# A transformer block on one core: token chunks of 2, 2, 4, 4 and 4 tiles instead of 2, 4, 4, 4 and 2, smaller idle products, and another written-out order

## The chip, the core and the metric

The kernel runs on one core of a Trainium2 chip. The metric is the device time of one execution in microseconds, as the median of several runs. The engines have short names: PE is TensorE (PEld its weight loads), DVE is VectorE, ACT is ScalarE, POOL is GpSimd, and SP only issues transfers.

## The reference, cut to what matters

2048 tokens with 448 features pass through an attention block with 16 heads of 28 features and then through a gated feed-forward block with 1792 inner features.

```python
def _A_ref(x, wqkv, w_phi, wo):
    q, k, v = split(x @ wqkv)                       # 16 heads of 28
    phi_q = concat([softmax(q @ w_phi), softmax(-(q @ w_phi))])
    phi_k = concat([softmax(k @ w_phi), softmax(-(k @ w_phi))])
    kv, z = einsum("bhsf,bhsd->bhfd", phi_k, v), einsum("bhsf->bhf", phi_k)
    o = (phi_q @ kv) / (phi_q @ z + 1e-6)
    return o.reshape(B, S, D) @ wo
def _B_ref(x, w_gate, w_up, w_down):
    return (sigmoid(x @ w_gate) * (x @ w_up)) @ w_down
h  = x + _A_ref(layernorm(x), wqkv, w_phi, wo)
h2 = h + _B_ref(layernorm(h), w_gate, w_up, w_down)
```

The sum over all tokens in kv stands between the two halves of the attention: no token can leave it before all tokens have gone into it.

## The kernel before, in words

The 2048 tokens are 16 tiles of 128. The kernel is a graph of tasks, each one or a few instructions on one engine; line 106 is the method that adds them. The order of all tasks is not found at run time: PLAN (line 30) is a list of task numbers written out by hand or by a search. `planned` (line 113) walks it, and `emit` (line 147) puts each task on its engine's queue in that order with semaphore waits for what it needs. A number with a tail such as `57.7-7` also says which of the eight PSUM banks the task writes; whoever takes a bank waits for those who last read it. A number with `~` takes the task's other engine. So an engine works strictly in the order of PLAN, and a task that waits holds up all that stand behind it on its engine, SP's transfers too.

The work runs in these stages.

- **Start** (lines 419 to 503). Five products with ones (L426) keep PE busy while the first weights land. Then the query and key weights are transposed on PE with a column that gives their mean (L445, "WT"), centred on ACT (L460), and folded with the small matrix w_phi (L475, "fold"); the folds leave PSUM by casts on ACT (L483) or DVE (L486). L491 ("csum") makes the column sums of the value weights. The first two token tiles are transposed on PE as well (L552, "xP"), the others by transfers (L363).
- **Keys and values** (lines 569 to 634). For each pair of tiles PE computes keys and values in half-array products (`pair`, line 520: two products of 64 rows run side by side, then called 64-row mode; all others use all 128 rows). ACT takes two exponentials of the key (L599) and a copy of the value (L604); DVE sums (L612) and inverts (L615); POOL, or DVE, multiplies ("phi", L619); PE adds into one bank over all tiles ("kv", L632). On DVE the multiplications with `lock=True` do not run beside POOL: line 126 makes each wait for POOL's task before it in PLAN, and POOL's next for it.
- **Queries** (lines 644 to 690). The same for queries, with POOL adding halves ("hs", L668), DVE reducing (L671), and POOL or DVE multiplying ("em", L681); a transfer turns each result ("eT", L689).
- **Leaving the attention** (lines 695 to 766). DVE copies the sums out ("kvz", L696). Then for each tile: the product with them ("num", L705), reciprocal and division on DVE (L713, "o" L715), a transpose (on PE for tiles 0 and 1, L723; by a transfer otherwise, "oT", L736), and the product with wo ("wo_", L750 for the first two tiles).
- **Second layernorm** (lines 768 to 815). DVE adds to the residual ("h", L770) and takes the statistics (L773, L775), POOL computes the factor (L776, L778, L789), ACT or DVE applies it ("hn", L791 or L793; L785 for the first two tiles), and a transpose brings it into the layout for PE ("hP" L800 and "hT" for tiles 0 and 1, by a transfer for pairs of tiles otherwise, "hT" L812).
- **Feed-forward** (lines 825 to 885). The tiles are taken in chunks given by SIZES (line 225). For each chunk, and for each of 14 blocks of 128 inner features, PE computes gate and up ("gu", also with `half`, L514) with 512 columns for a chunk of four tiles and 256 for one of two; ACT takes tanh (L848, "tg"), DVE multiplies (L855, "hh"). When all 14 blocks are there, each tile's product with w_down ("dn", L874) runs, DVE adds it to the residual ("fin", L881), and a transfer writes it out (L883). A chunk can start only when the "hT" of all its tiles have landed. The last two tiles are split in two column parts with `last` (line 861), so that less stands behind the last product.

Lines 817 to 820 make spare products with ones ("dm"). PLAN uses as many of them as it likes; they write a free bank and compute nothing.

Of the kernel before, what the change touches and what calls it, by code (L numbers as in the profile page):

```python
# [10 lines left out]
P = 128  # L11
# [19 lines left out]
23 24 25 26 27 28 29 30 31 32 33 34 35 36 37 38 39 40 41 42 0 20 18 21 16 17 6 14 8 49 4 57.7-7 58 59 60 61 654.0-0  # L31
64.0-0 3 65 9 5 15 43 1 11 10 44 2 51 46 45 48 47 55 73.1-1 74 19 22 66 75 67.2-2 70.3-3 68 69 120 71 72 118 119 121
12 62 63 122 7 13 123 124 167.4-4 94.5-5 165.6-6 97.7-7 88.0-0 98 95 89 91.1-1 92 99~ 90~ 96~ 166 168 93 112.2-2 113
169.3-3 171 173 175 170.6-6 172 174 176 193.0-7 79.4-4 180 179 127 125 115 128 114 126 182 80 183 187 186 177.1-5
194 189 132 190 136 133 138 134 137 139 135 178 76.2-2 195.3-6 129 130 131 184 116 191 140 117 141 198 181 81 197
188 205 204 185.4-4 85.1-1 196 211.0-5 206 199 82.7-7 192 212 213.3-6 77 200 142 86 201 207 83 208 215 216 87 218
145 219 147 143 146 149 148 144 150 202 209 220 151 152 214 84 78 217 229.0-1 222 203 230 234 223 224 225 226 227
153 231.2-7 233 210 240 236 106.3-3 232 100.5-5 107 108 235 241 101 247.0-6 221 242 102 248 251 103.3-3 109.2-2 104
252 154 237 243 244 156 254 255 157 158 160 159 161 155 238 110 228 249.1-7 250 111 105 239 265.0-5 260 258 245 259
253 319.2-3 266 270 269 320 256 162 163 246 261 262 263 164 257 272 276 277 327 328 273 279 274 267.6-7 283.0-1 268  # L40
271 284 329 280 287 288 330 290 291 278 321 322 281 331 285.3-5 286 301.0-6 302 264 275 335.2-7 282 336 292 294 295
306 305 289 293 323 297 298 324 308 312 313 315 309 316 332 299 325 310~ 317~ 326~ 54 56 50 52 53 334 333 296 338
337 303.0-1 353.3-6 304 314 344 307 345 354 370.2-5 300 363 355 311 356 362 318 455 387.0-1 461.7-7 388 346 339 347
462 348 340 463 364 365 341 366 397 371 372 519.4-4 404.3-6 389 390 464.7-7 456.0-0 465 520 515.7-7 349 357 358 457
458 359 350 342 367 343 360 459.0-0 405 521 379 373 460 522 406 407 414 380 413 516 421.0-2 543 361~ 544 368~ 517
352 351 369 545 537 546 538 539 469.4-4 547.3-3 422 518~ 470 540 548~ 541.5-5 466.7-7 471 381 467 382 468 374 375
423 542 430 431 655.6-6 656.6-6 694.3-6 695.4-5 696 697 698 396 424 700 476.2-2 473.7-7 699 702.3-6 703.0-1 704 705
477 474 478 475 376 701 710.2-7 711.4-5 712 713 706 708 391 398 383 377 707 716 714 709 378 384 385 399 392 717 715
400 393 415 401 402 394 395 472 479 523.3-6 438.0-1 524 525.4-5 439 526 549 556 550 551 557 564 571 558 386 718.2-7
719.3-6 720 721 441 447 440 448 726.0-4 727.1-5 728 729 724 722 565 723 725 566 572 408 552 553 559 554 560 561 567  # L50
568 730 732 555 562 573 731 733 574 416 575 569 576 734.2-7 735.3-6 736 737 403 738 740 570 742.0-4 743.1-5 744 745
563 746 739 577~ 741 748 747 749 483.2-2 487.7-7 480.3-3 490.6-6 753.0-0 481 484 488 482 409 432 433 491 489 410 578
756.1-4 757.3-5 758 759 760 762 425 754 485 417 449 492 764.0-7 765.2-6 766 767 768 426 427 761 434 770 442 450 443
444 451 428 763 445 435 452 411 772.1-4 773.3-5 774 775 776 769 778 771 418 446 419 429 436 412 779 780.0-7 781.2-6
782 783 777 784 786 785 787 493 486 788.3-5 789.1-4 790 791 529.0-7 527.2-6 792 794 793 795 530 528 796.3-5 797.1-4
798 799 601 586 579 594 602 580 603 800 802 803 581 604 605 801 804.6-7 805.0-2 806 807 808 810 420 497.1-1 498
494.4-4 495 809 811 437 606 582 583 584 453 454 750.3-3 501.5-5 499 496 585~ 502 587 588 589 590 591 503 595 596 597
598 607 592 599 600~ 500 818.6-6 504.7-7 815.0-0 816 511.2-2 512 505 513 819 508.1-1 531.4-5 821.0-0 532 593 509 751
506 510 616 617 822 609 610 608 824.2-6 825.3-7 826 827 830 611 831 828 829 507 514 832.1-5 833.0-4 834 835 836 838
837 839 840.3-7 841.2-6 842 843 844 845 618 612 613 614 619 620 846 847 848.1-5 849.0-4 850 851 820 752 533.3-7  # L60
535.2-6 852 854 534 536 855 624 631 856.0-4 857.3-7 858 859 639 625 626 853 646 647 860 862 615~ 863 648 861 640
# [155 lines left out]
def windows(ap):  # L217

    return bass.AP(ap.tensor, ap.offset, [list(ap.ap[0]), [192, 2], [1, 256]])


def build(nc, A_x, A_wqkv, A_w_phi, A_wo, B_w_gate, B_w_up, B_w_down, out):
    S = A_x.shape[1]
    NT = S // P
    SIZES = [2, 4, 4, 4, 2]
    CH = []
    for n in SIZES:
        t0 = CH[-1][0] + CH[-1][1] if CH else 0
        CH.append((t0, n))
    NB = len(CH)  # L230

# [7 lines left out]
    with ExitStack() as es:  # L239
# [5 lines left out]
        warm = sb("warm", [P, 512])  # L245
# [496 lines left out]
        for t in range(2):  # L742
# [4 lines left out]
            def f(e, t=t):  # L747
                b = got(("wx", t))[0]
                for k in range(4):
# [3 lines left out]
                 mode=128)  # L753
# [170 lines left out]
```

## Time and profile before

| | us |
|---|---|
| median of 3 runs (205.23 to 205.5) | 205.41 |
| the profiled execution | 206.85 |
| its span, first to last instruction | 205.0 |
| PE busy in it | 198.1 |
| DVE busy in it | 132.5 |
| ACT busy in it | 96.3 |
| POOL busy in it | 79.2 |

The profiled execution took 1.85 us more than its span; that lies before the first and after the last instruction. All times inside the kernel are counted from the first instruction. A busy PE is not a PE at its peak, since its products overlap: what matters is whether it had to wait before one.

### The profile page before, as it was taken

The page shows a single profiled execution, that of the slowest core. Times are in us where ns is not written, and L with a number is a line of the kernel's source. Part 1 is how long each engine was busy: PE and PEld are TensorE (multiplying, and loading weights), DVE is VectorE, ACT ScalarE, POOL GpSimd, SP SyncE. Part 2 cuts the span into 40 slices and gives each one's busy share as a digit, 9 for nine tenths or more (in the row PEclk, how much of TensorE's full clock was granted, in tenths as well). Part 3 has the DMA queues.
Part 4 walks back from the last instruction along what each step waited for, and adds up shares of the span by engine and source line. Part 5 has one row for each costly group of instructions (what it writes and reads, how often), then busy time and mean ns, then how long its engine had stood idle before and what let it go on. Part 6 is the DMA issues. An engine that isn't in the chain of part 4 may idle for free.

```text
span 205.0 us, 4981 instructions
## 1 busy us (share of the span) xinstructions
PE 198.1 (97%) x2026; PEld 108.4 (53%) x2027; DVE 132.5 (65%) x306; ACT 96.3 (47%) x182; POOL 79.2 (39%) x141
## 2 busy tenths in 40 slices
PE   6999999999999999999999999999999999999995
PEld 3645445444367784555555444444554444786563
DVE  2799799998999899735874775495204452642053
ACT  2768999999984570433231024236302334542000
POOL 7549899985758963560233011016000000000000
PEclk9999999999999999999999999999999999999999
DMA  5999999722466955509046570002202200000022
GB/s 138 265 260 206 286 353 364 289 58 54 78 130 102 159 109 47 102 16 191 3 83 115 86 189 0 3 2 51 56 0 84 37 2 0 3 3 0 0 93 90
DMA packets 49527, 21.06 MB, mean 103 GB/s; under 512 B 40288, under 2 KB 48480, under 8 KB 49504
## 3 DMA queue, kind: packets, MB, share of 16 engines
q1 hardware_dynamic: 49360, 20.71, 45.1%
q8 instruction: 16, 0.26, 0.5%
q14 instruction: 7, 0.06, 0.1%
q10 hardware_dynamic: 144, 0.03, 0.1%
HBM read 9.20 MB, written 1.84 MB: 54 GB/s over the span
## 4 chain that ended last, share of the span: by engine, by line
PE 79%; POOL 7%; DVE 5%; ACT 4%; DMA 2%; issue 1%
PE ps L514 51%; PE ps L874 20%; POOL halves L668 3%; DMA xT<-hn 2%; PE ps L632 2%; POOL eq L681 2%; ACT hh L460 1%; POOL rs L778 1%; PE ps L475 1%; PE ps L426 1%; DVE o_pad L715 1%; PE ps L585 1%; ACT hh L599 1%; ACT hh L604 1%; ACT eq L654 1%
## 5 line engine op out<-in xcount | busy, mean ns | idle before, releaser
L514 PE MATMUL ps<-xT,wg_sb 64*128 64x512 bf16 (+1 forms) x490 | 86.4, 333 | 0.7 <-DMA xT<-hn 0.4
L514 PE MATMUL ps<-xT,wu_sb 64*128 64x512 bf16 (+1 forms) x490 | 86.3, 333 | 0.0
L848 ACT ACTIVATE tg<-ps 128x512 f32<-128x512 f32 (+1 forms) x70 | 34.5, 510 | 84.5 <-PE ps L514 63.6
L855 DVE SCALAR_TENSOR_TENSOR hh<-tg,ps 128x512 bf16<-128x512 f32 (+1 forms) x70 | 38.3, 573 | 33.0 <-ACT tg L848 32.7
L514 PEld LDWEIGHTS ps<-xT,wg_sb 64*128 64x128 bf16 x490 | 45.6, 94 | 22.4 <-issue 1.9
L514 PEld LDWEIGHTS ps<-xT,wu_sb 64*128 64x128 bf16 x490 | 45.5, 94 | 15.2
L874 PE MATMUL ps<-wd_sb,hh 128*128 128x448 bf16 (+2 forms) x252 | 43.6, 332 | 0.3 <-DVE hh L855 0.3
L874 PEld LDWEIGHTS ps<-wd_sb,hh 128*128 128x128 bf16 x252 | 22.8, 98 | 19.5 <-issue 0.6
L881 DVE SCALAR_TENSOR_TENSOR x_sb<-ps,x_sb 128x448 bf16<-128x448 f32 (+2 forms) x18 | 9.9, 565 | 22.9 <-PE ps L874 22.9
L619 POOL TENSOR_TENSOR hh<-hh,rsum 128x896 bf16<-128x896 bf16 x14 | 23.6, 1698 | 1.3 <-DVE rsum L615 1.1
L654 ACT ACTIVATE eq<-ps,rs 128x448 bf16<-128x448 f32 x32 | 18.2, 647 | 3.2 <-PE ps L514 3.2
L599 ACT ACTIVATE hh<-ps,rs 128x448 bf16<-128x448 f32 x32 | 18.6, 647 | 2.3 <-PE ps L514 1.9
L776 POOL TENSOR_SCALAR rs<-mv 128x1 f32<-128x1 f32 x14 | 2.7, 191 | 40.3 <-DVE mv L775 39.7
L612 DVE TENSOR_REDUCE ssum<-hh 128x32 f32<-128x896 bf16 x16 | 17.0, 1062 | 1.8 <-ACT hh L599 1.6
L668 POOL TENSOR_TENSOR halves<-eq 128x448 f32<-128x448 bf16 x14 | 13.4, 969 | 8.5 <-DVE sq L671 4.4
L514 PE MATMUL ps<-Wvc,xT 64*128 64x448 bf16 x112 | 13.3, 351 | 0.2
L514 PE MATMUL ps<-Wq,xT 64*128 64x448 bf16 x112 | 13.0, 350 | 0.0
L514 PE MATMUL ps<-Wk,xT 64*128 64x448 bf16 x98 | 11.8, 350 | 0.4 <-ACT hh L460 0.2
L681 POOL TENSOR_TENSOR eq<-eq,rq 128x448 bf16<-128x448 bf16 x13 | 12.0, 938 | 0.3
L514 PE MATMUL ps<-wo_sb,oT 64*128 64x448 bf16 x98 | 10.4, 349 | 0.0
L604 ACT ACTIVATE hh<-ps,rs 128x448 bf16<-128x448 f32 x16 | 10.3, 654 | 0.1
L770 DVE TENSOR_TENSOR x_sb<-ps,x_sb 128x448 bf16<-128x448 f32 x14 | 8.1, 617 | 3.2 <-PE ps L514 3.2
(104 smaller groups left out, 189.4 us busy)
## 6 DMA issues: line engine op xcount, KB each, us to landing
wg_sb<-in_B_w_gate_dram SPq DMA_DIRECT2D x2, 896.0 KB, 8.3
wu_sb<-in_B_w_up_dram SPq DMA_DIRECT2D x2, 896.0 KB, 9.8
out_dram<-x_sb SPq DMA_DIRECT2D x14, 112.0 KB, 1.8
x_sb<-in_A_x_dram SPq DMA_DIRECT2D x3, 448.0 KB, 4.6
wd_sb<-in_B_w_down_dram SPq DMA_DIRECT2D x3, 448.0 KB, 10.2
hh<-in_A_wqkv_dram SPq DMA_DIRECT2D x4, 196.0 KB, 3.8
wo_sb<-in_A_wo_dram SPq DMA_DIRECT2D x2, 336.0 KB, 10.1
x_sb<-in_A_x_dram SPq DMA_DIRECT2D x2, 224.0 KB, 4.5
```

What stands on the lines that cost most here:

```text
L514: r = e.matmul(ap(), lhsT=st(blk, rows), rhs=mv(blk, rows), start=first and i == 0, stop=not first and i == 2, tile_position=(rows.start, 0))
L599: task((key, t), "act", 0.53, lambda e, t=t, s=s, i=i, b=kb: e.activation(signs(ek[:, s, :])[:, :, :, i, :], heads2(bank[b()][:, 0:D]), AC ...
L604: return e.activation(v1[:, t % NV, :, 0:DH], bank[b()][:, 0:D].rearrange("p (h d) -> p h d", d=DH), ACT.Copy, scale=rs1[:, 0, t:t + 1])
L612: task(("ss", t), "dve", 1.0, lambda e, s=s: e.tensor_reduce(ssum[:, s, :], ek[:, s, :].rearrange("p (h d) -> p h d", d=DH), AX.X, ALU.add ...
L619: return e.tensor_tensor(phi[:, t % NPHI, :, 0:GP].rearrange("p k (a d) -> p k a d", d=DH), ek[:, s, :].rearrange("p (k a d) -> p k a d", ...
L654: task((key, t), "act", 0.53, lambda e, w=w, t=t, i=i, b=bk[j]: e.activation(signs4(eq[:, w, :, 0:GP])[:, :, :, i, :], heads2(bank[b()][:, ...
L668: task(("hs", t), "pool", 0.9, lambda e, w=w, half_=half_, by4=by4: e.tensor_tensor(half_, by4(eq[:, w, :, 0:GP])[:, :, :, 0:DH // 2], by4 ...
L681: return e.tensor_tensor(ap, ap, rq[:, w, :].rearrange("p (k h) -> p k h", h=2)[:, :, :, None].to_broadcast([P, NPAIR, 2, DH]), ALU.mult)
L848: task(("tg", c, f_), "act", 0.51 if n == 4 else 0.3, lambda e, j=j, N=N, b=gb[i]: e.activation(tg[:, j % NSG, 0:N], bank[b()][:, 0:N], AC ...
L855: e.scalar_tensor_tensor(hhT[c % 2][:, f_, 0:N], tg[:, j % NSG, 0:N], 1.0, bank[b()][:, 0:N], op0=ALU.add, op1=ALU.mult), deps)
L874: r = e.matmul(bank[b][:, cols], lhsT=hhT[c % 2][:, f_, ts], rhs=wd_sb[:, f_, cols], start=(f_ == 0), stop=(f_ == FT - 1))
L881: e.scalar_tensor_tensor(X(t)[:, cols], bank[got(first)[0]][:, cols], 0.5, X(t)[:, cols], op0=ALU.mult, op1=ALU.add), [nm, ("hn", t)])
```

## The change

These things change.

- SIZES becomes 2, 2, 4, 4, 4. The first chunk is still tiles 0 and 1. The second is now tiles 2 and 3 alone, the others are 4 to 7, 8 to 11 and 12 to 15. There are as many products with 256 and with 512 columns as before.
- The spare products have 256 columns instead of 512, and there are 60 to choose from. The plan before used three of them (one ahead of the first WT, two ahead of the first gu); the new one uses six (two ahead of the first WT, one ahead of csum, three ahead of the first kv).
- `last` now means the tiles 14 and 15 whatever their chunk, so the same two tiles are split.
- PLAN is new. On PE, both xP now stand ahead of all folds (before, one fold stood between them). Two of the four WT of the query weights stand inside the first key products, and the others elsewhere than before. Products in 64-row and in 128-row mode change places 46 times instead of 54. Ahead of the first gu stands also the first half of the last query pair, and the second half follows four gu later; before, that pair came after twelve gu. The first gu of the second chunk follows straight on the last gu of the first; before, four num and a whole dn stood between. At the end come the dn of tiles 11, 8, 13, 9 and 12, mixed with the parts of 14 and 15.
- On ACT the centrings of the key weights that the first folds need come first, and one centring of query weights stands behind the first four exponentials; on DVE the sum (L612) of tile 5 stands ahead of three statistics (L533) that stood ahead of it before.
- On the other engines PLAN moves these too: three phi on DVE instead of two, the em of tile 0 on POOL instead of DVE, one em instead of two on DVE between kvz and the first gu (so one in all instead of three), the second cast ahead of the first gu ("hT" of tile 1) and the copy of h for tile 0 on ACT instead of DVE; on SP the loads of the feed-forward weights come in another order (the last is now a half of w_gate), and the last store is one of 28 KB on SP instead of ACT's.

```diff
 PLAN = """
-23 24 25 26 27 28 29 30 31 32 33 34 35 36 37 38 39 40 41 42 0 20 18 21 16 17 6 14 8 49 4 57.7-7 58 59 60 61 654.0-0
...
+16 14 17 0 18 11 23 24 25 26 27 28 29 30 31 32 1 43 33 46 34 35 36 37 38 39 40 41 20 3 42 53 55 56 49 48 4 19 21 44
...
-    SIZES = [2, 4, 4, 4, 2]
+    SIZES = [2, 2, 4, 4, 4]
...
-        for i in range(40):
-            task(("dm", i), "pe", 0.216, lambda e, i=i: e.matmul(
-                bank[got(("dm", i))[0]], lhsT=warm[:, 0:P], rhs=warm[:], start=True, stop=True), ["warm"], mode=128,
+        for i in range(60):
+            task(("dm", i), "pe", 0.108, lambda e, i=i: e.matmul(
+                bank[got(("dm", i))[0]][:, 0:256], lhsT=warm[:, 0:P], rhs=warm[:, 0:256], start=True, stop=True), ["warm"], mode=128,
                 banks=ANY, until=[("dm", i)], spare=True)
...
-                last = c == NB - 1
+                last = t >= NT - 2
```

More of the change, by code (lines that the diff above doesn't have):

```diff
@@ L36 @@
[L36 to L60, printed above, removed]
@@ new lines @@
+84 80 81 201 207 86 208 142 216 215 218 143 87 202 209 223 222 219 225 144 226 149 147 145 148 150 146 229.3-5
+213.0-6 214 192 100.1-1 101 203 220 217 102 103.7-7 227 104 230 210 109.2-2 106.0-0 107 110 224 231.1-6 232 233 234
+105 240 241 108 247.3-7 221 242 111 248 249.0-5 228 265.2-6 250 151 152 153 251 252 235 236 237 243 154 244 158 254
+238 258 259 155 255 261 159 262 156 160 157 161 245 266 239 319.1-3 320 246 256 253 260 270 269 328 276 277 322 321
+327 263 257 272 279 273 280 329 162 163 164 274 281 283.0-7 267.2-5 284 287 288 290 268 264 285.1-6 301.0-3 271 278
@@ new lines @@
+393 767 769 394 432 780 782 409 781 784.5-7 785.0-1 786 787 425 410 783 400 788 790 789 426 791 792.3-4 793.2-6 794
+795 796 427 798 433 417 797 799 401 395 442 402 449 800.5-7 801.0-1 802 803 804 806 807 805 808.3-4 809.2-6 810 811
+812 450 813 434 443 814 815 451 816.0-1 817.5-7 818 819 820 479 486 403 527.3-4 525.2-6 822 444 821 823 528 526
+824.0-1 825.5-7 826 827 830 828 586 587 571 564 588 565 579 829 572 573 566 580 490.4-4 487.6-6 770.2-2 428 411 418
+412 435 419 420 429 452 445 446 436 453 589 590 574 437 494.3-3 454 497.0-0 581 488 491 495 498 496 499 492 831 489
@@ new lines @@
+773.1-1 501.3-3 832.0-0 508.4-4 511.5-5 504.7-7 835.6-6 500 493 575 582 583 591 567 568 576 584 569 502 512 509 513
+774 505 510 503 836 506 833 771 592 585 570 577 531.1-5 529.3-4 532 530 593 578 838.6-7 839.0-2 840 841 609 842 594
+595 601 596 616 602 603 610 611 617 844 845 604 843 618 597 846.1-3 847.4-5 848 849 850 852 854.0-2 855.6-7 856 857
+851 853 612 619 620 860 605 598 613 614 599 858 621 606 607~ 861 859 600~ 862.1-3 863.4-5 864 865 870.6-7 871.0-2
+872 873 622 866 615 868 869 867 876 874 877 875 878.4-5 879.1-3 880 881 882 884 507 608 623 514 885 883 533.0-2
@@ L71 @@
+981 979 988 986 989 987 990.5-6 991.0-3 992 993 994 996 1006.1-7 1007.2-4 1008 1009 997 995 1010 1011 998.0-3
+999.5-6 1000 1001 1002 1003 1014.1-7 1015.0-3 1016 1017 1012 1004 1013 1005 1022.2-4 1023.5-6 1024 1025 1018 1019
+1028 1026 1020 1029 971.1-1 962.7-7 1021 1027 1033.5-5 1034 963 1040.6-6 965.0-0 1044.3-3 972 966 772 899 970 902
+905 837 1036.2-2 1037 1038 896 964 967 1039 1035 1030.4-4 1031 1032 1045 1048.5-5 1049 973 1046 1047 1050 1051 1041
+1042 1043
 """
```

34 lines of the change are left out of this document (20 added, 14 removed).

## The prediction

> **What bounds the kernel now.** I read the shares of the span first, then the busy times by stage, then the chain of work in order of time.
>
> ```profile
> span 205.0 us, 4981 instructions
> PE 198.1 (97%) x2026; PEld 108.4 (53%) x2027; DVE 132.5 (65%) x306; ACT 96.3 (47%) x182; POOL 79.2 (39%) x141
> PE 79%; POOL 7%; DVE 5%; ACT 4%; DMA 2%; issue 1%
> ```
>
> ```profile
> 0.00:10.30 10.30, 8.23 (x50) 5.18 (x51) 5.26 (x23) 5.30 (x9) 6.82 (x26) 1.00 0.90 202
> 10.30:48.10 37.80, 36.84 (x432) 18.16 (x432) 35.51 (x77) 35.11 (x67) 30.59 (x31) 1.00 0.89 246
> 48.10:59.50 11.40, 10.55 (x107) 4.70 (x107) 10.64 (x30) 10.46 (x21) 8.62 (x14) 1.00 0.61 115
> 59.50:79.80 20.30, 19.62 (x300) 14.25 (x300) 18.35 (x51) 10.66 (x25) 15.58 (x28) 1.00 0.75 107
> 79.80:202.70 122.90, 122.86 (x1140) 66.10 (x1140) 62.43 (x128) 34.76 (x63) 17.59 (x44) 1.00 0.23 48
> ```
>
> The columns of the stages are their length and the busy time of PE, PEld, DVE, ACT and POOL. From 79.80 to 202.70 PE is busy for 122.86 of 122.90 us, with DVE at half and ACT below a third: there nothing but the amount of PE work counts, and the change does not touch it (as many products of each width). From 10.30 to 79.80 the load is not on PE alone: in the second stage DVE is busy 94%, ACT 93%, POOL 81%, and an order of tasks decides who waits. So the change can gain or lose only ahead of 79.80, at the few changes of mode behind it, and at the very end.
>
> ```profile
> 3.82 0.43 PE ps L818
> 5.15 1.69 ACT hh L460 x3
> 6.97 0.35 PE ps L475 x2
> 7.32 0.43 PE ps L552 x4
> 7.75 1.31 PE ps L475 x14
> 9.05 1.49 PE ps L491 x4
> 10.54 1.88 PE ps L585 x8
> 33.99 0.56 PE ps L632 x16
> 41.86 0.34 PE ps L632 x8
> 75.52 4.19 DMA xT<-hn
> 79.84 23.98 PE ps L514 x224
> 202.75 0.27 DVE x_sb L881
> ```
>
> Columns of the chain: start, length, what. Three things are in it. First, four products of 448 columns take 1.49 us at 9.05 (0.37 each) and eight take 1.88 at 10.54 (0.24 each): PE runs at about half rate until some 10.5 us. (The clock column of the stages shows 1.00 there too; the lengths decide.) Second, eight kv products between two 64-row groups take 0.34, sixteen in one go 0.56. Eight more cost 0.22, so 0.34 holds about 0.12 for changes of mode; with one change seen on each group, I take 0.11 for each change. Third, the second chunk of gu begins at 79.84 on the landing of a transfer.
>
> **The change part by part.** The sum is made inside the profiled execution (206.85 us, span 205.0) and its difference is put on the median, 205.41.
>
> *Start.* This row of the timeline is the first xP:
>
> ```profile
> 5.84 0.63 PE L552 MATMUL ps<-ident,x_sb 128*128 128x128 bf16 x4
> ```
>
> It occupies PE for 0.43 (the other xP in the chain). So PE is empty from 6.27 to 6.97, when the first fold has the third centring (ACT's three end at 6.84), and the second xP comes afterwards. In the new order the two centrings that the first folds need come first on ACT (5.15 + 2 x 1.69/3 = 6.3), and the second xP fills the wait: the two end at 5.84 + 0.86 = 6.70. The folds start 0.27 earlier with 0.43 less to do among them: 0.7. The new spare product ahead of csum (half of the 0.43 of L818) takes 0.2 back: 0.5. I take 0.4 less, between 0 (the value weights or the casts are late anyway) and 0.7.
>
> *From the first keys to kvz, 10.30 to 48.10.* Rows of the groups and of the waits:
>
> ```profile
> L619 POOL TENSOR_TENSOR hh<-hh,rsum 128x896 bf16<-128x896 bf16 x14 | 23.6, 1698 | 1.3 <-DVE rsum L615 1.1
> L619 DVE TENSOR_TENSOR hh<-hh,rsum 128x896 bf16<-128x896 bf16 x2 | 2.1, 1088 | 0.1
> L681 DVE TENSOR_TENSOR eq<-eq,rq 128x448 bf16<-128x448 bf16 x3 | 1.8, 620 | 0.0
> DVE ssum L612 <- ACT hh L599: 1.6, 3, 1.2
> ```
>
> DVE gets a third phi (1.09) and loses the em of tile 0 (0.62): 0.47 more on the engine that sets kvz (it has 35.51 busy of 37.80). Against that, POOL's phi waited 1.1 for DVE's reciprocals and DVE waited 1.6 for ACT. In the new order the sum of tile 5 on DVE stands ahead of three statistics that stood ahead of it before, and one centring of query weights goes into ACT's hole after the first four exponentials. If all of these waits go, the stage is 1.6 - 0.47 = 1.1 shorter; if none goes, 0.5 longer. The six fewer changes of mode ahead of the first gu (6 x 0.11 = 0.66) count here only where PE is the last to come, and I put no sum on them. I take 0.5 less, a little above the middle of -1.1 and +0.5, since ACT's hole is filled for sure.
>
> *From kvz to the first gu, 48.10 to 59.50.* This is one chain through DVE, PE, ACT and POOL, tile by tile.
>
> ```profile
> L673 DVE RECIPROCAL rq<-sq 128x16 f32<-128x16 f32 x16 | 3.4, 227 | 0.1
> L757 DVE CAST x_sb<-ps 128x448 bf16<-128x448 f32 x1 | 0.6, 615 | 0.0
> L809 DVE CAST xT<-ps 128x512 bf16<-128x512 f32 x1 | 0.7, 684 | 0.0
> L756 ACT CAST x_sb<-ps 128x448 bf16<-128x448 f32 x1 | 0.5, 539 | 0.0
> L806 ACT CAST xT<-ps 128x512 bf16<-128x512 f32 x1 | 0.6, 576 | 0.0
> ```
>
> DVE is busy 10.64 of 11.40 here. Between kvz and the last "hn" that the first gu needs, DVE loses two reciprocals (0.45), one em (0.62), one cast of h (0.62) and one cast of hT (0.68): 2.4 us, of which about 0.4 was overlap with the next instruction, so 2.0. ACT gets the two casts, 0.54 + 0.58 = 1.1, and it is busy 10.46 of 11.40. If DVE alone sets the pace, the stage is 2.0 shorter; if ACT does, nothing is won. New behind hP stands a query product of 0.9, which lies beside the cast on ACT. I take 1.2 less, nearer to DVE's end, because the chain goes through DVE four times for each tile and ACT's exponentials in it can be done later.
>
> *From the first gu to the last product.* Before, two stalls stand around the dn that fills the wait for the second chunk:
>
> ```profile
> 76.60 2.38 PEld L874 LDWEIGHTS ps<-wd_sb,hh 128*128 128x128 bf16 x14 [0.37 <-DVE hh L855]
> 79.81 0.09 PEld L514 LDWEIGHTS ps<-xT,wg_sb 64*128 64x128 bf16 x1 [0.82 <-issue]
> ```
>
> They make 1.2. The 0.9 of the query product has left this stretch, and two changes of mode fewer make 0.2: 2.3 less if nothing new waits. What is late next is the second chunk itself: its gu follow the first chunk's with no dn in between. From the first gu on PE has 98 pairs of gu products (59.51 to 59.62 is one, so 0.11 each, 10.7), half a query pair (0.6), one wo_ pair (1.3), four num (0.9) and four changes of mode (0.4): 13.9 us. Meanwhile POOL must come to the last "nb" of tile 3:
>
> ```profile
> 59.51 0.28 PE L514 MATMUL ps<-xT,wu_sb 64*128 64x256 bf16 x1
> 59.62 0.27 PE L514 MATMUL ps<-xT,wg_sb 64*128 64x256 bf16 x1
> L668 POOL TENSOR_TENSOR halves<-eq 128x448 f32<-128x448 bf16 x14 | 13.4, 969 | 8.5 <-DVE sq L671 4.4
> L681 POOL TENSOR_TENSOR eq<-eq,rq 128x448 bf16<-128x448 bf16 x13 | 12.0, 938 | 0.3
> L675 POOL TENSOR_TENSOR rq<-rq,sq 128x16 f32<-128x16 f32 x16 | 3.3, 220 | 2.7 <-DVE rq L673 2.7
> L778 POOL TENSOR_TENSOR rs<-rs,neghalf 128x1 f32<-128x1 f32 x16 | 8.8, 551 | 3.0 <-DVE eq L681 1.3 <-DVE rs L776 0.7
> L789 POOL TENSOR_SCALAR nb<-mv,rs 128x1 f32<-128x1 f32 x14 | 3.6, 265 | 1.1
> DMA to landing us min/median/max: 3.1/3.2/4.8
> ```
>
> In the new order POOL does five hs (4.85), four em (3.75), four rq (0.9) and two factors (2 x (0.55 + 0.27 + 0.2) = 2.0) there: 11.5 us, which may begin when DVE's second hn is through, some 1.4 us ahead of the first gu (one hP and one cast before it). So the last nb comes 10.1 us after the first gu, then DVE's hn (0.4) and the transfer (3.1 to 4.8, the last row, of L812): landing at 13.6 to 15.3 against 13.9. I take 0.7 of wait, and 0.5 for the first hh of the small chunks, which a bank waits for: 1.2. Bounds 0 and, if POOL is held up, several us (a rival below). Net 2.3 - 1.2 = 1.1 less; I write 1.0. The third chunk has room: between the last wo_ of tiles 4 to 7 and its gu lie four dn at 2.65 and two wo_ pairs, some 16 us, against about 14 for statistics, four hn and two transfers.
>
> *End.* Last product, DVE's 0.27, one store of 28 KB: the same chain, from SP instead of ACT. Nothing, within 0.1.
>
> Sum: -0.4 - 0.5 - 1.2 - 1.0 = -3.1, so 205.41 - 3.1 = **202.3 us**.
>
> **A rule against the row.** PE's lengths double in speed at about 10.5 us, 3.5 us after its last gap (6.3 to 6.97). The Trainium skill's page "TensorE: Matmul & The Clock Gate", section "Part 1: The HAM clock gate", has PE at half clock until one window of about 3.4 us is busy, with windows that run freely. By that rule, and the trace agrees, filling the gap at 6.3 could let an earlier window count.
>
> **The rivals.**
>
> 1. *The clock rises a window earlier.* The gap at 6.3 is filled, so full speed could come near 7 us instead of 10.5. Folds and csum behind 7.1 would take half of their 3.4 us; the casts of the folds on DVE then come last and leave about 0.9 of the 1.7. Time: 202.3 - 0.9 = 201.4. Against it: the trace shows a single rise, and not where an earlier window would have ended.
> 2. *ACT takes DVE's place ahead of the first gu.* The 1.1 us of casts fall on an engine that is 92% busy there. Then the third term is 0 and the second too: 205.41 - 0.4 - 1.0 = 204.0.
> 3. *The second chunk starves* (slower). Before, POOL's hs alone waited 4.4 us for DVE's reductions (row of L668). If POOL meets such waits between the first gu and the last nb, the landing comes at 18 to 19.7 instead of 13.6 to 15.3, and with no dn ahead of the second chunk PE stands still for about 5 us instead of the 1.2 counted. Time: 202.3 + 3.9 = 206.2. It decides from a wait of 4.3 us at that place on, where it has eaten the whole 3.1. Against it: DVE has less to do in the stage before, and POOL has fewer tasks ahead of the last nb.
> 4. *It does nothing.* The chunks hold the same products, and spare products only fill holes; if each hole moves to the next one, 205.4.
>
> **How the numbers follow.** A measurement of this kernel tells about 0.2% (0.4 us) from no change. Chances: the forecast 0.46 (its own range 200.9 to 203.6, from the bounds of its terms), the early clock 0.12, ACT 0.14, nothing 0.05, the starved chunk 0.23. So faster 0.72, same 0.05, slower 0.23. Half of the early clock's and about half of the starved chunk's chance may lie outside: the range is 200.7 to 206.2.
>
> **What would show it.** Right: the first csum near 8.4; the first gu near 57.5 instead of 59.51; the second chunk's first gu some 14 to 15 us behind it with a wait of under 1.5 us on the transfer of hn; PE without a break from there; the last product near 199.5. Wrong: half-clock lengths ending near 7 (rival 1), casts of ACT in the chain ahead of the first gu (rival 2), PE waiting over 4 us on the transfer with POOL's halves waiting on DVE (rival 3). A gap at the third chunk's first gu would break the claim that everything behind the second chunk is PE's alone.

## The result, and the profile after

| | before | after |
|---|---|---|
| median, us | 205.45 (4 runs, 205.23 to 205.57) | 202.11 (4 runs, 201.98 to 202.38) |
| ratio to before | | 0.984 (95%: 0.9823 to 0.9857) |
| profiled execution, its span | 206.85, 205.0 | 201.98, 200.3 |
| a second profiled execution of before, its span | 205.44, 203.7 | |

After is 3.3 us faster. The profile that the prediction was made from does not show a usual execution of before: it took 1.4 us more than the median. Apart from two far outliers (229 and 1122 us), 75 executions of before are on record: 55 between 205.1 and 206.2 us and 20, this profile among them, between 206.4 and 207.0; the four of the table all belong to the lower group, so a ratio from another session can differ by some 0.2%. In the second profile, 205.44 us, PE doubles its rate 5 us earlier, and the kernel is 1.38 us ahead of the first at the phi of tile 12 and 1.32 at its last product. So after is held against the second profile from here on: spans 203.7 and 200.3, a difference of 3.4 that agrees with the medians.

The page of after: span, busy time of each engine, and the chain's shares. (After's PLAN is a line longer than before's, so in the views of after a line has a number one higher: its L515 is L514 of before.)

```profile
span 200.3 us, 4990 instructions
PE 195.1 (97%) x2030; PEld 105.0 (52%) x2030; DVE 130.4 (65%) x304; ACT 95.5 (48%) x183; POOL 79.1 (39%) x142
PE 84%; ACT 7%; POOL 3%; DVE 3%; issue 1%
```

Windows of before's second profile, cut at the first key product, at kvz, at the first gu, at the second chunk's first gu and at the last DVE operation (length, then busy PE, PEld, DVE, ACT, POOL, granted clock, DMA share, GB/s):

```profile
0.00:9.05 9.05, 6.39 (x50) 3.67 (x51) 4.61 (x22) 5.30 (x10) 6.83 (x26) 1.00 0.82 207
9.05:46.72 37.67, 36.70 (x431) 18.11 (x433) 35.96 (x78) 34.97 (x67) 30.65 (x32) 1.00 0.92 252
46.72:58.13 11.41, 10.62 (x108) 4.70 (x107) 10.65 (x30) 10.49 (x21) 8.64 (x14) 1.00 0.63 115
58.13:78.52 20.39, 19.67 (x300) 14.29 (x301) 18.40 (x51) 10.67 (x25) 15.68 (x28) 1.00 0.71 107
78.52:201.43 122.91, 122.87 (x1140) 66.17 (x1140) 62.40 (x129) 34.79 (x63) 17.63 (x44) 1.00 0.23 49
```

The same cuts in after:

```profile
0.00:8.64 8.64, 6.29 (x53) 3.75 (x53) 4.28 (x21) 5.10 (x9) 6.70 (x26) 1.00 0.82 208
8.64:46.48 37.84, 37.49 (x442) 18.64 (x443) 36.34 (x80) 36.32 (x69) 30.20 (x33) 1.00 0.94 261
46.48:56.28 9.80, 9.72 (x107) 4.51 (x105) 9.16 (x25) 9.80 (x20) 7.19 (x11) 1.00 0.28 54
56.28:70.83 14.55, 14.45 (x250) 11.18 (x251) 12.05 (x35) 8.82 (x21) 10.76 (x19) 1.00 0.83 117
70.83:198.01 127.18, 127.14 (x1188) 66.94 (x1183) 68.33 (x147) 35.41 (x66) 24.23 (x56) 1.00 0.30 54
```

Read the lengths first: -0.41, +0.17, -1.61, and for the last two together -1.57. The sum is -3.42. Then read PE against each length: before it stood idle for 0.97, 0.79 and 0.72 us of the three middle stages, in after for 0.35, 0.08 and 0.10. In after PE has something to do at nearly every point from the first key product to the end, and so most of what is left there of changes of mode and waits counts in the total.

Busy time hides the changes of mode, because the ends of products are modelled. So the next table goes by starts: "products" is the sum of the distances that products have back to back (0.189 us for 448 columns, 0.109 for 256, 0.216 for 512), and "rest" is what the stage takes beyond it. The changes are counted in the order of PE's work. The cut is at the last kv here instead of at kvz, since that is PE's.

| stage, from start to start | before: length = products + rest, changes | after |
|---|---|---|
| first key product to last kv | 37.23 = 31.25 + 5.98, 30 | 37.40 = 32.34 + 5.06, 26 |
| last kv to first gu | 11.85 = 8.88 + 2.97, 13 | 10.24 = 8.45 + 1.79, 11 |
| first gu to second chunk | 20.39 = 18.67 + 1.72, 4 | 14.55 = 13.49 + 1.06, 4 |
| second chunk to last product | 122.36 = 121.57 + 0.79, 7 | 126.64 = 126.00 + 0.64, 5 |

The rest fell by 0.92 + 1.18 + 0.66 + 0.15 = 2.91 us. The eight changes of mode that are gone are worth 0.85 of it (0.106 each, measured below); the other 2.06 are put down to waits of PE, and its idle time in the windows above agrees: it fell by 1.95 in the three middle stages. The first key product comes 0.41 earlier, and 0.1 of spare products went from these stages into the start.

Two rows of before show such waits, one ahead of the first gu and one on the transfer that the second chunk needs:

```profile
58.13 0.27 PE L514 MATMUL ps<-xT,wg_sb 64*128 64x256 bf16 x1 [0.27 <-DVE rden L713]
78.52 0.37 PE L514 MATMUL ps<-xT,wg_sb 64*128 64x512 bf16 x1 [0.42 <-DMA xT<-hn]
```

The first row names a reciprocal of DVE that ended just then, but by the kernel the first gu does not need it. It needs the casts of hT, and the later of the two, on ACT in before, ends at 57.89:

```profile
57.31 0.58 ACT L806 CAST xT<-ps 128x512 bf16<-128x512 f32 x1
```

In after neither first product has a wait in its brackets. The first gu starts when the query product ahead of it leaves PE, and the second chunk's first product (70.83) follows the last one of the first chunk:

```profile
56.28 0.27 PE L515 MATMUL ps<-xT,wg_sb 64*128 64x256 bf16 x1
...
70.83 0.27 PE L515 MATMUL ps<-xT,wu_sb 64*128 64x256 bf16 x1
```

### The profile page after: what moved, and what is told of

Same layout as the page of the kernel before. It is cut to its first block, busy times and chain, and to the rows that moved or that the text cites. A ratio compares the mean times of both kernels' runs of the same rounds, so it can differ in the third digit from the quotient of the medians.

```text
span 200.3 us, 4990 instructions
## 1 busy us (share of the span) xinstructions
PE 195.1 (97%) x2030; PEld 105.0 (52%) x2030; DVE 130.4 (65%) x304; ACT 95.5 (48%) x183; POOL 79.1 (39%) x142
## 4 chain that ended last, share of the span: by engine, by line
PE 84%; ACT 7%; POOL 3%; DVE 3%; issue 1%
PE ps L515 55%; PE ps L875 21%; ACT hh L600 3%; POOL hh L620 2%; ACT hh L605 2%; PE ps L706 2%; PE ps L633 1%; PE ps L427 1%; ACT Wq L484 1%; PE ps L586 1%; PE ps L446 1%; ACT hh L461 1%; DVE sq L672 1%; DVE st L534 1%; POOL halves L669 0%
## 5 line engine op out<-in xcount | busy, mean ns | idle before, releaser
L515 PE MATMUL ps<-xT,wg_sb 64*128 64x512 bf16 (+1 forms) x490 | 86.6, 333 | 0.0
L515 PE MATMUL ps<-xT,wu_sb 64*128 64x512 bf16 (+1 forms) x490 | 86.5, 333 | 0.0
L849 ACT ACTIVATE tg<-ps 128x512 f32<-128x512 f32 (+1 forms) x70 | 33.9, 510 | 73.6 <-PE ps L515 70.5
L515 PEld LDWEIGHTS ps<-xT,wg_sb 64*128 64x128 bf16 x490 | 45.4, 94 | 22.6 <-DVE hh L856 1.2
L515 PEld LDWEIGHTS ps<-xT,wu_sb 64*128 64x128 bf16 x490 | 45.3, 94 | 15.8
L620 POOL TENSOR_TENSOR hh<-hh,rsum 128x896 bf16<-128x896 bf16 x13 | 21.8, 1699 | 0.2 <-DVE rsum L616 0.2
L655 ACT ACTIVATE eq<-ps,rs 128x448 bf16<-128x448 f32 x32 | 19.0, 691 | 0.0
L682 POOL TENSOR_TENSOR eq<-eq,rq 128x448 bf16<-128x448 bf16 x15 | 13.8, 939 | 0.3
L515 PE MATMUL ps<-Wvc,xT 64*128 64x448 bf16 x112 | 13.1, 350 | 0.1
L515 PE MATMUL ps<-Wq,xT 64*128 64x448 bf16 x112 | 13.1, 351 | 0.1
L515 PE MATMUL ps<-Wk,xT 64*128 64x448 bf16 x98 | 11.7, 350 | 0.0
L515 PE MATMUL ps<-wo_sb,oT 64*128 64x448 bf16 x98 | 10.3, 350 | 0.1
L792 ACT ACTIVATE hn<-x_sb,nb,rs 128x512 bf16<-128x512 bf16 x9 | 7.1, 808 | 6.8 <-POOL nb L790 6.8
```

Source lines behind the costliest of these rows:

```text
L515: r = e.matmul(ap(), lhsT=st(blk, rows), rhs=mv(blk, rows), start=first and i == 0, stop=not first and i == 2, tile_position=(rows.start, 0))
L620: return e.tensor_tensor(phi[:, t % NPHI, :, 0:GP].rearrange("p k (a d) -> p k a d", d=DH), ek[:, s, :].rearrange("p (k a d) -> p k a d", ...
L655: task((key, t), "act", 0.53, lambda e, w=w, t=t, i=i, b=bk[j]: e.activation(signs4(eq[:, w, :, 0:GP])[:, :, :, i, :], heads2(bank[b()][:, ...
L682: return e.tensor_tensor(ap, ap, rq[:, w, :].rearrange("p (k h) -> p k h", h=2)[:, :, :, None].to_broadcast([P, NPAIR, 2, DH]), ALU.mult)
L849: task(("tg", c, f_), "act", 0.51 if n == 4 else 0.3, lambda e, j=j, N=N, b=gb[i]: e.activation(tg[:, j % NSG, 0:N], bank[b()][:, 0:N], AC ...
```

## Experiments

Ratios are to before, timed in the same session; after's own is 0.984. Two theories stand against each other. **O** (the prediction's): between the first keys and the first gu the other engines set the pace, by their loads and waits. **P**: PE itself sets it, so that a kernel's time is PE's products plus changes of mode plus waits, stage by stage.

### Before again

No edit.

> The kernel before, unchanged, for a second profile of it. The profiled execution of before took 206.85 us, 1.4 more than its median, and its products ran at half rate until 10.5 us (csum 1.49 us); in after they run at full rate from 5.3 us (csum 0.81). If the moment at which the rate doubles wanders from execution to execution (theory W), this second profile may show csum at 0.8 and a span near 203.5. If the start of before itself makes it late (theory S: the break of PE at 6.3 us), csum is 1.49 again at the same place and the span is 205.0. The median is 205.4 within 0.3 either way.

Measured: 205.39 us (10 runs, 205.21 to 206.67), ratio 0.9978 (0.9957 to 1.0), span 203.7. The products of csum (L491; duration min/median/max), first in the profile that the prediction used:

```profile
L491 PE MATMUL ps<-hh,ones x3: 581/581/581, 8.8 to 10.0; 128*128 128x448 bf16 x3
```

and in this one:

```profile
L491 PE MATMUL ps<-hh,ones x3: 351/353/355, 7.9 to 8.5; 128*128 128x448 bf16 x3
```

The same program, with the same break of PE ahead of its folds, runs csum at half rate in one execution and at full rate in the other. Theory W holds: the moment wanders. Its worth is 1.38 us, and it was in the prediction's base. Beside the 1.38, the order of the work and its waits are the same in both.

### Only the new start

Before, with this edit of the order:

```diff
-PLAN up to csum as in before
+PLAN up to csum as in after
```

> Before, with only the order up to csum taken from after (first stationary and centring orders, second xP ahead of the folds, three spare products of 256 columns instead of one of 512). The prediction's first term says 0.4 less: 205.0. If the rate doubles earlier because of this order (theory S), csum is near 0.81 long and starts near 8 us in every profile, and the kernel is 0.9 to 1.4 faster: 204.0 to 204.5. If the moment wanders by itself (theory W): 204.8 to 205.3 whatever this profile shows.

Measured: 206.36 us (12 runs, 206.19 to 206.53), ratio 1.0023 (1.0004 to 1.0041): a miss on the other side. csum does run at full rate, but the first key product comes at 10.01 instead of 9.05. The chain of this kernel says why:

```profile
7.65 2.23 DVE Wk L486 x4
9.88 0.14 issue
10.01 1.99 PE ps L585 x8
```

All four casts of the folded key weights stand on DVE. Before has one of the four on ACT and the new order another one, which lies behind csum; this kernel takes the other three from the new order and leaves that one where before had it, on DVE. With that cast on ACT, six other kernels with after's start (the next one and five further below) begin their keys at 8.78 to 8.99. So the new start gains nothing without that cast on ACT.

### Only the new order ahead of the first gu

After's PLAN ahead of the first gu (without the query product that stands last there), before's chunks and before's order behind it:

```diff
-    SIZES = [2, 2, 4, 4, 4]
+    SIZES = [2, 4, 4, 4, 2]
```

> After's order of all work ahead of the first gu product (its start, statistics, casts, exponentials), and behind it before's chunks of 2, 4, 4, 4 and 2 tiles in before's order; the query product that after has ahead of the first gu stays behind it. By the prediction's terms the head is worth 0.4 + 0.5 + 1.2 = 2.1: 203.3 us. By the two traces it is worth 3.2 less what the late clock of the profiled before makes (up to 1.4): 1.8 to 3.2, so 202.3 to 203.7. Rival: the chunk sizes carry the gain (fewer stalls behind the first gu), and the head only moves waits: 204.4 or more.

Measured: 211.85 us (6 runs), ratio 1.0282 (1.0251 to 1.0313). The first gu comes at 56.63, 1.50 ahead of before's 58.13, as the new order promises. Then PE stands still. Waits from 60 to 66 us (engine, line, waited for; us, times, longest), and windows there:

```profile
PE ps L705 <- DMA eqT<-eq: 3.9, 1, 3.9
```

```profile
56.63:60.00 3.37, 1.88 (x28) 1.22 (x28) 2.56 (x8) 2.33 (x6) 1.10 (x3) 1.00 0.02 5
60.00:63.00 3.00, 0.00 (x0) 0.00 (x0) 0.31 (x1) 0.29 (x2) 1.89 (x2) 0.74 1.06 199
63.00:66.00 3.00, 2.69 (x34) 2.13 (x36) 1.95 (x7) 0.00 (x0) 0.19 (x1) 0.50 0.34 63
```

Before's order does the num of tiles 4 and 5 right behind the first gu, and had made their em ahead of it. The new order does those em later, here from 57.76 to 58.92. So num waits for their transfer, PE runs dry, and its clock falls to half (the column before the last two). The 1.5 us of the head are real, but only the order behind it can keep them.

### Only the new chunks

Before's order ahead of the first gu, after's chunks and order behind it, and one query half put in between:

```diff
-    SIZES = [2, 4, 4, 4, 2]
+    SIZES = [2, 2, 4, 4, 4]
```

> Before's order of all work ahead of the first gu product, and behind it after's chunks of 2, 2, 4, 4 and 4 tiles in after's order (the spare product of 512 columns of the start as two of 256, and one query half put ahead of the first gu, which PE does beside the cast it waits for). By the prediction's last term the chunks are worth 1.0: 204.4 us; by the traces 1.5: 203.9. If head and chunks add up, this gain and that of the kernel with the new head alone make 3.3 together. Rival: in this order POOL comes later to the last nb of tile 3 and the second chunk starves (its transfer lands over 1.5 us after the first chunk's last product): 205 or more.

Measured: 207.38 us (6 runs), ratio 1.0081 (1.005 to 1.0111). The rival's size, by another mechanism: one stall lies just ahead of the first gu (59.88), the other inside the first chunk.

```profile
59.12 0.93 PE L514 MATMUL ps<-Wq,xT 64*128 64x448 bf16 x8 [0.89 <-DVE o_pad L715]
```

```profile
65.44 0.74 PE L514 MATMUL ps<-wo_sb,oT 64*128 64x448 bf16 x6 [1.55 <-DVE hh L855]
```

The query half takes a bank that a division on DVE has to free, and a product with wo waits for a bank that an hh on DVE has to free. Grafted like this, neither half of the change gains alone. An order searched anew for the old chunk sizes was not run, so whether the gain needs the new sizes stays open.

### Spare products where the other engines are loaded

After, with a spare product of 256 columns between two 64-row products at six places from 28.9 to 40.8 us, here the first:

```diff
 PE: vp of tiles 8 and 9, second half
+PE: dm, 256 columns
 PE: kp of tiles 10 and 11, second half
```

> After, with six more spare products of 256 columns between 64-row products from 28.9 to 39.5 us, each into a bank that is free there: 6 x 0.11 of products and twelve more changes of mode. The prediction took DVE, ACT and POOL to set the pace of this stage (theory O): then PE has room and kvz, the first gu and the end move by 0 to 0.4 us: at most 202.5. If PE itself sets it (theory P), all counts: 6 x 0.11 + 12 x 0.10 = 1.9 later from the sixth on, 204.0.

Measured: 203.62 us (6 runs), ratio 0.99 (0.9866 to 0.9934). From the first key product to the last kv it takes 38.48 us against 37.40 in after; the stages behind have their old lengths (10.29, 14.52, 126.64). So 1.1 of the 1.9 count, and 0.8 vanish in waits that were there anyway. That is between the theories and nearer to P.

### The same spare products among gu

```diff
 PE: four gu of the third chunk
+PE: dm, 256 columns
 PE: four gu of the third chunk
```

and so on, six times in the third and the fourth chunk.

> After, with the same six spare products between the gu products of the third and fourth chunk, where PE has no gap: 6 x 0.11 of products and twelve more changes of mode at 0.10 to 0.11 make 1.9: 204.0 us. This is the price list for the kernel with the six in the middle. If a change of mode costs nothing of its own there (the weight load behind it is hidden), only the products count: 202.8.

Measured: 204.14 us (6 runs), ratio 0.9919 (0.9888 to 0.995). The third and the fourth chunk, from first gu to first gu, in this kernel:

```profile
99.55:124.31 24.76, 24.76 (x229) 10.92 (x227) 14.68 (x29) 9.43 (x16) 3.83 (x12) 1.00 0.31 53
124.31:159.87 35.56, 35.56 (x271) 16.25 (x268) 16.09 (x31) 9.43 (x16) 3.92 (x12) 1.00 0.11 23
```

and in after:

```profile
99.45:123.25 23.80, 23.80 (x226) 10.94 (x224) 14.68 (x29) 9.43 (x16) 3.83 (x12) 1.00 0.34 55
123.25:157.85 34.60, 34.60 (x268) 16.29 (x265) 16.09 (x31) 9.43 (x16) 3.93 (x12) 1.00 0.11 23
```

0.96 more in each, 1.92 in all. Six products are 6 x 0.109 = 0.65; the other 1.27 is twelve changes of mode at 0.106.

### Two casts back on DVE

```diff
-h of tile 0 and hT of tile 1: cast on ACT
+h of tile 0 and hT of tile 1: cast on DVE
```

> After, with the casts of h of tile 0 and of hT of tile 1 on DVE, as before had one of each there (1.2 us more for DVE, 1.1 less for ACT ahead of the first gu). The prediction's third term (DVE sets the pace between kvz and the first gu) makes the first gu about 1.1 later: 203.2. If PE's own products set it (theory P: PE is busy from 44.8 to 56.3 without a gap over 0.2), the move fits in: 0 to 0.3 later, 202.1 to 202.4. If ACT sets it (rival 2), it is faster than after.

Measured: 203.24 us (5 runs), ratio 0.9882 (0.9848 to 0.9917), as the prediction's term says. From the last kv to the first gu it takes 11.42 us instead of 10.24, with the same products and changes of mode. Waits from 46 to 58 us in this kernel:

```profile
PE ps L514 <- DVE xT L809: 0.7, 1, 0.7
...
PE ps L800 <- DVE rs L776: 0.6, 1, 0.6
```

PE waits 0.7 for the cast and 0.6 for the first hn, which the other cast holds up. So here theory P fails where it said that a loaded PE leaves room: PE was busy 9.72 of 9.80 us, and DVE was just in time. Both are tight there: 1.2 us more on DVE made the stage 1.18 longer.

### A dn between the first two chunks

```diff
 PE: last gu of the first chunk
+PE: dn of tile 0
 PE: first gu of the second chunk
...
-PE: dn of tile 0
 PE: dn of tile 1
```

With it move, on DVE, the last two hh of the chunk and the addition of tile 0, and on SP its store.

> After, with the first dn put between the first and the second chunk's gu, where before had one. The prediction's stalls: dn waits 0.4 for the last hh and the second chunk starts with up to 0.8 of wait, and two changes of mode more make 0.2: 0.6 to 1.4 more, 202.7 to 203.5. If before's stalls came from something else than this dn, only the changes of mode count: 202.3.

Measured: 206.96 us (12 runs), ratio 1.0058 (1.0036 to 1.0081): 4.9 above after, more than either side said. Waits from 70 to 100 us:

```profile
PE ps L874 <- DVE hh L855: 1.5, 1, 1.5
...
PE ps L705 <- DVE x_sb L770: 1.0, 1, 1.0
PE ps L705 <- DVE hh L855: 0.9, 1, 0.9
```

The dn waits for the last tanh and the last product on DVE of its own chunk, as expected. The surprise is behind the second chunk. There this dn had filled PE's time; now two num wait. The first waits for a bank that DVE's addition of the residual (L770) frees. For the second the row names an hh, but by the kernel it needs the transfer of the queries of tiles 12 and 13, which was issued at 89.12 and landed at 95.34; this num starts at 95.48. The rest grows by 1.80 up to the second chunk (2.86 against 1.06) and by 2.63 behind it (3.27 against 0.64).

### No spare products

```diff
-PLAN: dm.0 and dm.1 ahead of the first WT, dm.2 ahead of csum, dm.3 to dm.5 ahead of the first kv
```

> After without its six spare products (two ahead of the first WT, one ahead of csum, three ahead of the first kv; 0.11 us each). Where they lie PE waits for a load, a cast and a phi anyway, so without them nothing starts earlier or later: 202.1, within 0.2; the prediction's first term counted 0.2 for the one ahead of csum, which would make it 201.9. If they hold up the moment at which the rate of PE doubles, products at half rate show beyond 7 us in this profile and it takes up to 1.4 more: 203.5.

Measured: 202.65 us (6 runs, 201.84 to 203.03), ratio 0.9839 (0.9807 to 0.9871): after's ratio, but a median 0.54 above after's, and 0.35 above the upper end of what was expected. csum runs at full rate and the first key product comes at 8.70 instead of 8.64. The profiled execution is 1.05 behind after's at its last product. 0.72 of that is one transfer: o of tiles 2 and 3 landed 4.70 us after its issue, in after 3.98.

```profile
PE ps L514 <- DMA oT<-o_pad: 0.7, 1, 0.7
```

So the spare products cost nothing, and whether they are worth nothing or up to half a microsecond these runs do not tell.

### POOL late for the second chunk

```diff
+        scr = sb("scr", [P, 1536])
+        task("late", "pool", 1.85, lambda e: e.memset(scr[:], 0.0))
```

with its place in PLAN ahead of the variance of tile 2.

> After, with one more memset of about 1.3 to 1.9 us on POOL ahead of the variance of tile 2 (computes nothing that is used). The prediction's third rival: the second chunk waits for the last nb. In after its transfer lands 0.58 us ahead of the chunk's first product, so the chunk begins the memset's length less 0.6 later, 0.7 to 1.3, and since PE has no gap behind it the end is as much later: 202.8 to 203.4. If something else has room there (the memset fits into POOL's waits): 202.1 to 202.3.

Measured: 203.41 us (6 runs), ratio 0.9881 (0.9849 to 0.9913). The memset takes 1.38 us, and the stage from the first gu to the second chunk takes 15.87 instead of 14.55: all but 0.06 of it counts, though the expectation left 0.6 of room. Rows of DVE and of PE show where:

```profile
68.09 0.41 DVE L793 TENSOR_SCALAR hn<-x_sb,rs,nb 128x512 bf16<-128x512 bf16 x1 [1.36 <-POOL nb L789]
68.42 0.41 DVE L855 SCALAR_TENSOR_TENSOR hh<-tg,ps 128x256 bf16<-128x256 f32 x1
```

```profile
68.89 0.28 PE L514 MATMUL ps<-xT,wg_sb 64*128 64x256 bf16 x1 [0.84 <-DVE hh L855]
```

PE does not wait on the transfer of hn at all. DVE waits for the last nb in its queue, an hh of the first chunk stands behind it, and a gu waits for the bank that this hh frees. The transfer then lands 0.54 ahead of the second chunk's first product, as in after (0.58).

### Two other orders

Both keep after's chunks and its start, and were searched with the lengths of after's profile. The first:

```diff
-phi of tile 14 on DVE, em of tile 3 on DVE, hn of tile 3 on DVE
+phi of tile 14 on POOL, em of tile 3 on POOL, hn of tile 3 on ACT
-oT of tiles 0 and 1 and v1 of tile 10 on ACT, em of tiles 5 and 9 on POOL
+oT of tiles 0 and 1 and v1 of tile 10 on DVE, em of tiles 5 and 9 on DVE
...
-PE: keys of tiles 0 and 1, then of tiles 2 and 3
+PE: keys of tiles 2 and 3 first, those of tiles 1 and 0 among and behind them
```

> After with another order of the work from the first keys to the second chunk, the chunks and everything else as in after: the order was searched with the lengths that the profile of after shows for each task and 0.105 us for each change of mode. It has 50 changes of mode against 46, but fewer waits of PE; phi of tile 14 goes to POOL, casts of oT to DVE. If PE's waits and changes of mode are all that is left to gain ahead of the second chunk (theory P), it is 0.5 to 1.0 faster than after: 201.1 to 201.6. If small waits that those lengths do not tell eat the gain, it is even with after (202.1) or slower.

Measured: 208.34 us (6 runs), ratio 1.012 (1.0079 to 1.0161). Waits from 8 to 18 us:

```profile
ACT hh L599 <- PE ps L585: 7.3, 1, 7.3
...
PE ps L514 <- DMA xT<-in_A_x_dram: 2.2, 1, 2.2
```

The keys of tiles 2 and 3 wait for a load, ACT's first exponential for the keys behind them, and the clock of PE drops (0.84 from 11.09 to 21.50). The search had not held the first keys to their load. The second order keeps them in place:

```diff
-phi of tile 14 on DVE, em of tile 3 on DVE, hn of tile 3 on DVE
+phi of tile 14 on POOL, em of tile 3 on POOL, hn of tile 3 on ACT
-oT of tiles 0 and 1, hT of tile 1, v1 of tiles 12 and 13 on ACT
+oT of tiles 0 and 1, hT of tile 1, v1 of tiles 12 and 13 on DVE
```

> After with another order of the work from the first keys to the second chunk, chunks and start up to csum as in after; searched with the lengths of the profile of after, 0.105 us for each change of mode (48 of them against 46), and for each transposing transfer one of the longest landings that the runs show (for o of tiles 2 and 3: 4.6 us, 4.0 in after). The two halves of that wait are the point: phi of tile 14 on POOL, both casts of oT and the cast of hT of tile 1 on DVE, so that the o of tiles 2 and 3 is through earlier. By those lengths the first gu comes where it does in after and the second chunk 0.1 to 0.7 earlier: 201.4 to 202.1. If PE's waits ahead of the second chunk are used up already (no order has much less), it is even with after: 202.1; waits that those lengths do not tell make it slower, as in the order before.

Measured: 204.0 us (6 runs), ratio 0.9909 (0.9885 to 0.9933). By stages, as in the table above: 38.05, 10.67 and 14.96 against 37.40, 10.24 and 14.55, 1.5 more. In its profile the value weights land late as well (this wait is that execution's own):

```profile
PEld ps L491 <- DMA hh<-in_A_wqkv_dram: 1.1, 1, 1.1
```

No order tried here beats after.

## Why the prediction was right, step by step

- **The base.** The terms were made inside an execution that ran at half rate until 10.5 us. Since they were differences, most of them survived. The second profile is what they should have been held against.
- **Start, 0.4 less: met in one pair of executions, not settled.** The first key product comes 0.41 earlier (9.05 to 8.64) when both executions have the early clock. But in the six other kernels with after's start it comes at 8.78 to 8.99, and with only the new chunks, where the start is before's up to the size of a spare product, at 8.88; so part of the 0.41 is these two executions' own. The path was also another than in the sum: csum starts 0.11 earlier (7.94 to 7.83), since the folds now stand still in their middle until 7.33 for ACT's last centring, and the other 0.30 is a cast that the first key product waited for in before. The start alone, with one cast left on the wrong engine, loses 1.0 at the same place.
- **First keys to kvz, 0.5 less: wrong.** The stage took 0.17 more. The failed step is that DVE sets kvz, so that what DVE loses and waits for sets the stage. PE already had work for 36.70 of 37.67 us, and in after for 37.49 of 37.84; six spare products among this work made the stage 1.1 longer. These rows are kvz, in before's second profile and in after:

```profile
46.72 0.64 DVE L696 TENSOR_TENSOR kvz<-ps,maskP 112x464 bf16<-112x464 f32 x1
46.48 0.64 DVE L697 TENSOR_TENSOR kvz<-ps,maskP 112x464 bf16<-112x464 f32 x1 [0.49 <-PE ps L633]
```

  In before DVE comes to kvz from an em, just as PE has done the last kv; in after DVE stands 0.49 and waits for PE. The new order does save 0.92 of rest there, with four changes of mode fewer, but spends it on 1.09 more of products ahead of the last kv: half of a query pair (0.57) and a product of tile 0 (0.19) that before did later, and three spare ones (0.33). The gain shows up where that work is missing, one stage later. The six changes ahead of the first gu, on which the prediction put no sum, are 0.6 of the total.
- **kvz to the first gu, 1.2 less: right, and mis-sized by 0.4.** It is 1.61. The two casts put back on DVE cost 1.18, so DVE does set the pace at these places, and rival 2 (ACT takes its place) is out: the stage is shorter although ACT is busy 9.80 of 9.80 us. By the table it is 1.18 less rest, and 0.43 less products: 1.19 went, most of it to the stage before, and the query half of 0.76 came.
- **First gu to the last product, 1.0 less: right in sign, by other terms.** It is 1.57: the query product moved out (0.76) and 0.81 less rest. The 1.2 us of new waits did not come. The landing was predicted 13.6 to 15.3 us behind the first gu and came after 13.97; PE was there after 14.55, not after 13.9, and did not wait. Of the 1.2 of stalls that were to go, about half shows (rest 1.72 to 1.06): the term took 0.82 from a row of weight loads, while PE itself stood for 0.42 at that place (the row at 78.52). So two sizes were too large, the stalls that go and the waits that come, and they partly made up for each other.
- **End, nothing: right.** From the start of the last product to the end of the span it is 2.5 us in both, and the execution is the span plus 1.7 in both.
- **0.11 for a change of mode: right,** 0.106.
- **Rival 1, the early clock:** it is real, but it is no gain of the change's median, since before has it in its usual executions too.
- **Rival 3, the second chunk starves:** it did not happen, but the place was well chosen. There is next to no room: 1.38 us more on POOL made 1.32 more in all. The wait comes through DVE's queue and a bank, not through the transfer.
- **Rival 4, nothing:** out by 3.3 us.
- **The sum, 3.1 for 3.3 measured: in part luck.** The second term missed by 0.7 on one side, the third and the fourth by 0.4 and 0.6 on the other. The range 200.9 to 203.6 is not what the bounds of the terms add up to: the lower ones alone (0.7, 1.1, 2.0 and 2.3) give 199.3.

The four kernels with a part of the change or with one dn moved are all slower than before. So neither the chunk sizes nor a part of the order gains when it is put into an order made for the other. What the stages show is that PE finds something to do at nearly every point, the second chunk's gu straight behind the first's among it. Two things stay open. One is whether a new order alone, with the old chunk sizes, would have gained as much. The other is how much of the 2.06 us of waits belongs to which single move of the order; only the casts (1.18) and the place of the dn (4.4) were priced alone, as what undoing them in after costs, which need not be what they brought.

## What to carry to other kernels

Where an engine has work for 93% or more of every stage, count its rest: starts against back-to-back distances, with a price for each change of mode. A stage that gets no shorter may have done work for the next one. And an order is made for its chunk sizes: each part of this change, grafted on the rest of before, lost 0.2 to 2.8%.

## What the runs showed of the hardware that was not expected

The moment at which PE's products double their rate, read from the distances of products in the profiles here: between 4.4 and 7.0 us in 13 of them (4.9 in after), and 10.5 in the first profile of before. That is one step of about 3.4 us past 7.1, and just ahead of that PE had stood idle from 6.27 to 6.97. A step of this length shows in the granted clock of the first of the two other orders, which is half from 12.47 to 15.88, and twice its length in the kernel with only the new head, from 61.42 to 68.25. The Trainium skill's page "TensorE: Matmul & The Clock Gate", section "Part 1: The HAM clock gate", has a free-running window of that length, which agrees. With the new start, the orders whose rate doubled latest (6.7 with only the new start, 6.8 with only the new head, 7.0 with the dn in between) had products almost back to back up to there, so none of them lost a window. That the new start excludes the late case is argued from this, not shown; that the 12 executions with only the new start lie within 0.34 us, while before's two groups are some 1.2 apart, speaks for it.

Pauses at full rate, from the start of a product to the start of the next: 1.2 us (5.75 to 6.93 in before's second profile) and 1.8 (63.62 to 65.44 with only the new chunks) did not bring the half rate back. One of 2.5 us (8.57 to 11.09 in the first of the two other orders) was followed by it at 12.47, and during one of 4.2 us (59.12 to 63.31 with only the new head) it came at 61.42.

One and the same transfer, o of tiles 2 and 3, landed 3.98 us after its issue in after and 4.70 in the kernel without spare products, and PE waited for it there. Over all profiles here it took 3.04 us (spare products where the other engines are loaded) to 4.80 (the second of the two other orders).
